# Attention with a cluster mask and an MLP on one Trainium2 core: the value product taken four heads at a time, sums from a pass of ones, and queries in halves

## The chip, the cores and the metric

The kernel runs on one core of one Trainium2 chip. The metric is the device time of one execution in microseconds (us). The core has five engines that run their own instruction lists in order: TensorE (PE; its weight loads are shown as PEld), VectorE (DVE), ScalarE (ACT), GpSimd (POOL) and SyncE (SP), which here only starts transfers. Data is in SBUF and PSUM (128 partitions each; PSUM has eight banks of 512 f32 per partition), and sixteen DMA engines move it.

## The reference

Four batches of eight heads, 768 positions, 64 dimensions, 16 centroids per head. Every query and key is given to the centroid with the largest cosine; a query sees only keys of its own cluster.

```python
q_assign = np.argmax(np.einsum('bhsd,hcd->bhsc', q_n, c_n), axis=-1)
k_assign = np.argmax(np.einsum('bhsd,hcd->bhsc', k_n, c_n), axis=-1)
mask = q_assign[:, :, :, None] == k_assign[:, :, None, :]
scores = scale * np.matmul(q, k.transpose(0, 1, 3, 2))
scores = np.where(mask, scores, -1e9)
attn = np.exp(scores - max); attn = attn / attn.sum(-1)
x = np.matmul(attn, v)                    # to 3072 tokens x 512
h = x @ w_in                              # 512 x 2048
out = (h * sigmoid(h)) @ w_out            # 2048 x 512
```

(The last lines are shortened; all inputs and the output are float32.)

## The kernel before

The order of the work is written out by hand: the tile scheduler is off, and each engine runs what the program emits for it in that order. A head has six key blocks of 128.

**Preparation of a head.** load_qk brings q and k of one head (192 KB each), load_v its v; POOL casts v to f16 into vts (line 83), of which the other 64 columns hold ones. On DVE, hi and lo (lines 91, 97) split q and k, times 128, into a high and a low f16 part; xpose (line 107) transposes both by a DMA into ab, so that a column of ab has the high part in partitions 0 to 63 and the low part in 64 to 127. logits (line 117) multiplies by the centroids: eight matmuls, whose outputs are 32 partitions each, so that q and k in groups of three blocks stand below each other in one PSUM tile. am_t, am_max, am_back (lines 127 to 143) turn it, take the maximum and make a one-hot code, and codes (lines 152, 154) writes the code into partitions 64 to 79 of ab, over the low part: times 16384 for queries, times 16384 minus 16384 for keys. The score matmul over 80 partitions then carries the mask.

**Attention.** A step is one key block j of one head i: qk_mm (lines 163, 164) makes scores for 128 keys and all 768 queries in two matmuls of 512 and 256 columns, exp (line 170) turns them into P on ACT. pv_mm (line 178) multiplies vt (128 columns: 64 of v, 64 of ones) by P, a half of the queries at a time, with six matmuls of 384 columns; half of the output partitions are the value product, the other half the sum of P. evac (line 187) copies it to SBUF on DVE. The sums go through transfers: one row to zt as 128x6, reciprocal there (line 197), out to DRAM (rzd), and back as a broadcast to 64 partitions (rzb, line 206); norm (line 214) on POOL multiplies and writes xt, f16, feature by token, two heads to a tile.

**MLP.** unit_a (line 233) makes 128 of the 2048 hidden features for one half of a batch in four matmuls of 384 columns, with tanh on ACT (line 237) and a product on DVE (line 238), since h sigmoid(h) = h (1 + tanh(h / 2)) / 2; unit_aa (line 252) does the same for both halves at once in the last batch. unit_b (line 272) makes 128 tokens of the output in sixteen matmuls of 512 columns, with a copy on DVE (line 277) and the transfer out.

**Order.** In step j of head i PE gets: the scores of the next step, at j = 3 the logits of head i + 2, a unit A at j = 0, 1, 2, 4, a unit B at j = 5, and three value matmuls of head i - 1 at j = 0, 1, 3, 4. The units of a batch are put in the queue at head 2 of the next batch (so at heads 10, 18, 26). Preparation runs three to six heads ahead. The weights are loaded in eight transfers on POOL's queue (w_load), behind a small copy (pace) that waits for an exp. Fillers (line 296) keep PE running in the first heads. After the last head the rest of the MLP follows.

PSUM: two slots of two banks (st: scores, phs), three of one bank (mm: psL, ph, po), one (pv: pO).

Of the kernel before, what the change touches and what calls it, by code (L numbers as in the profile page):

```python
# [12 lines left out]
ALU = mybir.AluOpType  # L13
AX = mybir.AxisListType


@with_exitstack
def kernel(
# [15 lines left out]
    NT = B * S  # L34
# [3 lines left out]
    NBH = B * H  # L38
    HALF = S // 2
    assert D == 64 and DM == H * D and S == 768 and HC == 16 and H == 8  # L40
# [4 lines left out]
    NV = 8  # L45
# [4 lines left out]
    drpool = ctx.enter_context(tc.tile_pool(name="drpool", bufs=1, space=bass.MemoryType.DRAM))  # L50
# [5 lines left out]
    xts = [const.tile([128, NT], f16, name=f"xt{r}") for r in range(NR)]  # L56
    vts = [const.tile([128, NJ, 128], f16, name=f"vt{n}") for n in range(NV)]
    stk = const.tile([128, H, 32], f16, name="stk")
    ckl = const.tile([128, H, 32], f16, name="ckl")
    ohp = [const.tile([128, 12, 32], f16, name=f"oh{n}") for n in range(2)]  # L60
    pace = const.tile([128, 1], f32, name="pace")
    zz = const.tile([128, 512], f16, name="zz")

    nat, hls, abs_, psLs, LTs, mxs, ohs, Ps, pOs, osbs, zts, rzds, rzbs, pst = ({} for _ in range(14))

    def per_head(f):
        return lambda i, *a: f(i, *a) if 0 <= i < NBH else None

    @per_head
    def load_qk(i):  # L70
        b, h = divmod(i, H)
        qk = mp.tile([128, 2, NJ * D], f32, name="qk", bufs=3)
        nc.sync.dma_start(qk[:, 0, :], q[b, h].rearrange("(p j) d -> p (j d)", j=NJ))
        nc.sync.dma_start(qk[:, 1, :], k[b, h].rearrange("(p j) d -> p (j d)", j=NJ))
        nat[i] = qk

    @per_head
    def load_v(i):
        b, h = divmod(i, H)
        vn = mp.tile([128, NJ, D], f32, name="vn", bufs=3)  # L80
        nc.sync.dma_start(vn, v[b, h].rearrange("(p j) d -> p j d", j=NJ))
        lo = 0 if i % 2 == 0 else 64
        nc.gpsimd.tensor_copy(vts[i % NV][:, :, lo : lo + D], vn)  # L83

    @per_head
    def hi(i, t=slice(0, 2)):
        if i not in hls:
            hls[i] = mp.tile([128, 2 * NJ, 2, D], f16, name="hl", bufs=3)
        hl = hls[i].rearrange("p (t j) c d -> p t j c d", t=2)
        src = nat[i].rearrange("p t (j d) -> p t j d", d=D)  # L90
        nc.vector.tensor_scalar(out=hl[:, t, :, 0, :], in0=src[:, t], scalar1=QS, scalar2=None, op0=ALU.mult)  # L91

    @per_head
    def lo(i, t=slice(0, 2)):
        hl = hls[i].rearrange("p (t j) c d -> p t j c d", t=2)
        src = nat[i].rearrange("p t (j d) -> p t j d", d=D)
        nc.vector.scalar_tensor_tensor(  # L97
            out=hl[:, t, :, 1, :], in0=src[:, t], scalar=QS, in1=hl[:, t, :, 0, :], op0=ALU.mult, op1=ALU.subtract
        )

    @per_head
    def xpose(i, parts=1):
        hl = hls.pop(i)
        ab = mp.tile([128, 2 * NJ, 128], f16, name="ab", bufs=5)
        n = 2 * NJ // parts
        for t in range(parts):
            nc.sync.dma_start_transpose(ab[:, t * n : t * n + n, :], hl[:, t * n : t * n + n].rearrange("p n c d -> p (n c d)"))
        abs_[i] = ab

    @per_head  # L110
    def logits(i):
        h = i % H
        ab = abs_[i]
        psL = ps.tile([128, HALF], f32, name="psL", tag="mm", bufs=3)
        for w, st in ((stk, True), (ckl, False)):
            for g in range(4):
                nc.tensor.matmul(  # L117
                    psL[32 * g : 32 * g + 32, :], w[:, h, :],
                    ab[:, 3 * g : 3 * g + 3, :].rearrange("p n c -> p (n c)"),
                    start=st, stop=not st,  # L120
                )
        psLs[i] = psL

    @per_head
    def am_t(i):
        LT = mp.tile([128, 12, 32], f32, name="LT", bufs=2)
        nc.vector.transpose(LT.rearrange("p n c -> p (n c)"), psLs.pop(i))
        LTs[i] = LT

    @per_head  # L130
    def am_max(i):
        LT = LTs.pop(i)
        mx = mp.tile([128, 12], f32, name="mx", bufs=2)
        nc.vector.tensor_reduce(out=mx, in_=LT[:, :, 0:HC], axis=AX.X, op=ALU.max)
        oh = ohp[i % 2]
        nc.vector.tensor_tensor(
            out=oh[:, :, 0:HC], in0=LT[:, :, 0:HC], in1=mx.unsqueeze(2).to_broadcast([128, 12, HC]), op=ALU.is_ge
        )

    @per_head  # L140
    def am_back(i):
        ohT = mp.tile([128, HALF], f16, name="ohT", bufs=2)
        nc.vector.transpose(ohT, ohp[i % 2].rearrange("p n c -> p (n c)"))
        ohs[i] = ohT

    @per_head
    def codes(i):
        ohT, ab = ohs.pop(i), abs_[i]
        for g in range(4):
            dst = ab[64 : 64 + HC, 3 * g : 3 * g + 3, :].rearrange("p n c -> p (n c)")  # L150
            if g < 2:
                nc.vector.tensor_scalar(out=dst, in0=ohT[32 * g : 32 * g + HC, :], scalar1=OHV, scalar2=None, op0=ALU.mult)
            else:
                nc.vector.tensor_scalar(  # L154
# [364 lines left out]
```

## Time and profile before

| what | us |
|---|---|
| median of three runs | 394.45 |
| the three runs | 393.79, 398.59, 394.45 |
| span of the profiled execution | 393.8 |
| first exp starts | 15.0 |
| first tanh starts | 102.5 |
| last unit B starts its stretch of 96 matmuls | 368.9 |
| DMA queue 1 (loads, transposes, outputs) | 44.29 MB |

The profiled execution took what the fastest of the runs took; its span is that time. The page of the profile gives each engine's busy time, the span in 40 slices (a digit is the busy share in tenths), the chain of work that ended last, and groups of instructions with count, busy time and mean. A matmul's duration has its way through the array in it, so matmuls that follow each other overlap, and their price is read from start to start.

### The profile page before, as it was taken

The page shows a single profiled execution, that of the slowest core. Times are in us where ns is not written, and L with a number is a line of the kernel's source. Part 1 is how long each engine was busy: PE and PEld are TensorE (multiplying, and loading weights), DVE is VectorE, ACT ScalarE, POOL GpSimd, SP SyncE. Part 2 cuts the span into 40 slices and gives each one's busy share as a digit, 9 for nine tenths or more (in the row PEclk, how much of TensorE's full clock was granted, in tenths as well). Part 3 has the DMA queues.
Part 4 walks back from the last instruction along what each step waited for, and adds up shares of the span by engine and source line. Part 5 has one row for each costly group of instructions (what it writes and reads, how often), then busy time and mean ns, then how long its engine had stood idle before and what let it go on. Part 6 is the DMA issues. An engine that isn't in the chain of part 4 may idle for free.

```text
span 393.8 us, 5826 instructions
## 1 busy us (share of the span) xinstructions
PE 344.9 (88%) x2001; PEld 174.6 (44%) x2001; DVE 266.4 (68%) x591; ACT 205.5 (52%) x310; POOL 98.4 (25%) x148
## 2 busy tenths in 40 slices
PE   8759977774687999987999999989999999977995
PEld 3224434432344555543555455445555545443442
DVE  6868877895489987792778877785666345256421
ACT  4337946754477755572666666565557514044300
POOL 3111164365133222222212401250223205000000
PEclk9859989998699999998999999999999999999999
DMA  5796899999868955560555555534310102200022
GB/s 137 189 252 161 198 182 225 195 200 221 144 138 170 227 122 127 130 187 11 147 149 147 123 147 149 145 85 89 87 49 21 49 28 89 80 1 2 1 79 80
DMA packets 82125, 48.84 MB, mean 124 GB/s; under 512 B 62128, under 2 KB 76464, under 8 KB 82096
## 3 DMA queue, kind: packets, MB, share of 16 engines
q1 hardware_dynamic: 79408, 44.29, 46.3%
q0 software_dynamic: 2688, 4.19, 7.0%
q8 instruction: 15, 0.25, 0.3%
q14 instruction: 14, 0.11, 0.1%
HBM read 33.59 MB, written 6.39 MB: 102 GB/s over the span
## 4 chain that ended last, share of the span: by engine, by line
PE 65%; DVE 13%; DMA 12%; ACT 4%; SPq 2%; issue 2%; POOL 1%; DVEq 0%; ACTq 0%; POOLq 0%
PE po L272 21%; PE ph L233 13%; PE pO L178 12%; PE pS L163 8%; DMA qk<-in_k_dram 7%; DMA rzb<-rzd 4%; PE pS L164 3%; PE phs L252 3%; PE junk L296 3%; DVE osb L187 2%; DVE gt L262 2%; DVE gt L238 2%; PE psL L117 2%; DMA rzd<-rz 2%; ACT tn L260 1%
## 5 line engine op out<-in xcount | busy, mean ns | idle before, releaser
L170 ACT ACTIVATE P<-pS 128x768 f16<-128x768 f32 x192 | 149.8, 809 | 34.3 <-PE pS L164 33.8
L237 ACT ACTIVATE tn<-ph 128x384 f32<-128x384 f32 x96 | 47.2, 491 | 102.4 <-PE ph L233 97.3
L178 PE MATMUL pO<-P,vt 128*128 128x384 f16 x384 | 85.7, 334 | 14.9 <-DVE osb L187 14.5
L233 PE MATMUL ph<-xt,win_s 128*128 128x384 f16 x384 | 78.2, 327 | 11.5 <-POOL xt L214 11.5
L272 PE MATMUL po<-wout_s,gt 128*128 128x512 f16 x384 | 87.0, 383 | 0.0
L163 PE MATMUL pS<-ab 80*128 80x512 f16 x192 | 75.9, 396 | 10.0 <-DVE ab L154 5.1
L214 POOL TENSOR_TENSOR xt<-osb,rzb 64x384 f16<-64x384 f32 x64 | 64.3, 1024 | 54.1 <-DMA rzb<-rzd 40.5
L238 DVE SCALAR_TENSOR_TENSOR gt<-tn,ph 128x384 f16<-128x384 f32 x96 | 53.0, 552 | 35.3 <-ACT tn L237 33.4
L178 PEld LDWEIGHTS <-vt 128*128 128x128 f16 x384 | 36.8, 99 | 58.9 <-issue 38.2
L83 POOL CAST vt<-vn 128x384 f16<-128x384 f32 x32 | 18.4, 575 | 174.0 <-DMA vn<-in_v_dram 160.0
L272 PEld LDWEIGHTS <-gt 128*128 128x128 f16 x384 | 38.0, 99 | 44.8 <-issue 2.1
L164 PE MATMUL pS<-ab 80*128 80x256 f16 x192 | 53.6, 279 | 0.0
L277 DVE TENSOR_SCALAR ot<-po 128x512 f32<-128x512 f32 x24 | 16.6, 692 | 53.4 <-PE po L272 53.4
L233 PEld LDWEIGHTS <-win_s 128*128 128x128 f16 x384 | 37.2, 97 | 26.3 <-issue 0.6
L187 DVE COPY osb<-pO 128x384 f32<-128x384 f32 x64 | 35.2, 550 | 2.5 <-PE pO L178 1.9
L97 DVE SCALAR_TENSOR_TENSOR hl<-qk,hl 128x768 f16<-128x768 f32 (+1 forms) x33 | 33.0, 1000 | 0.2
L163 PEld LDWEIGHTS <-ab 80*128 80x128 f16 x192 | 19.0, 99 | 23.0 <-DVE ab L154 6.3
L164 PEld LDWEIGHTS <-ab 80*128 80x128 f16 x192 | 19.4, 101 | 22.1 <-issue 8.3
L91 DVE TENSOR_SCALAR hl<-qk 128x768 f16<-128x768 f32 (+1 forms) x33 | 20.4, 618 | 11.2 <-DMA qk<-in_k_dram 5.8
L252 PE MATMUL phs<-xt,win_s 128*128 128x384 f16 x128 | 22.2, 327 | 5.2 <-DVE gt L262 5.2
L260 ACT ACTIVATE tn<-phs 128x768 f32<-128x768 f32 x16 | 13.0, 811 | 25.0 <-PE phs L252 25.0
L296 PE MATMUL junk<-zz 128*128 128x512 f16 x80 | 24.8, 436 | 1.2 <-DVE zz L312 1.2
(48 smaller groups left out, 199.4 us busy)
## 6 DMA issues: line engine op xcount, KB each, us to landing
qk<-in_q_dram SPq DMA_DIRECT2D x32, 192.0 KB, 3.4
qk<-in_k_dram SPq DMA_DIRECT2D x32, 192.0 KB, 3.2
vn<-in_v_dram SPq DMA_DIRECT2D x32, 192.0 KB, 3.9
rzb<-rzd SPq DMA_DIRECT2D x32, 192.0 KB, 4.0
out_dram<-ot SPq DMA_DIRECT2D x24, 256.0 KB, 2.2
win_s<-in_moe_w_in_dram POOLq DMA_DIRECT2D x4, 512.0 KB, 7.5
wout_s<-in_moe_w_out_dram POOLq DMA_DIRECT2D x4, 512.0 KB, 7.6
ab<-hl SPq DMA_TRANSPOSE x33, 3.8
```

The lines of the kernel that those rows point to most:

```text
L163: nc.tensor.matmul(pS[:, 0:512], lhsT, ab[0:80, 0:4, :].rearrange("p n c -> p (n c)"), start=True, stop=True)
L164: nc.tensor.matmul(pS[:, 512:768], lhsT, ab[0:80, 4:6, :].rearrange("p n c -> p (n c)"), start=True, stop=True)
L170: nc.scalar.activation(out=P, in_=pst.pop((i, j))[:, 0:S], func=AF.Exp, bias=0.0, scale=ESC)
L178: nc.tensor.matmul(pOs[i], vts[i % NV][:, j, :], Ps[i, j][:, c * HALF : c * HALF + HALF], start=(j == 0), stop=(j == NJ - 1))
L187: nc.vector.tensor_copy(osb[:, c * HALF : c * HALF + HALF], pOs.pop(i))
L214: nc.gpsimd.tensor_tensor(out=xts[h // 2][o : o + 64, b * S + c * HALF : b * S + c * HALF + HALF], in0=osbs[i][o : o + 64, cs], in1=rzbs[i ...
L233: nc.tensor.matmul(ph, win_s[:, r, ts(fb, 128)], xts[r][:, T0 : T0 + HALF], start=(r == 0), stop=(r == NR - 1))
L237: nc.scalar.activation(out=tn, in_=ph, func=AF.Tanh, bias=0.0, scale=0.5)
L238: nc.vector.scalar_tensor_tensor(out=gt[:, fb, :], in0=tn, scalar=1.0, in1=ph, op0=ALU.add, op1=ALU.mult)
L252: nc.tensor.matmul(phs[:, 512 * c : 512 * c + HALF], win_s[:, r, ts(fb, 128)], xts[r][:, T0 : T0 + HALF], start=(r == 0), stop=(r == NR - 1),)
L272: nc.tensor.matmul(po, gt[:, fc, ts(t, 128)], wout_s[:, fc, :], start=(fc == 0), stop=(fc == NFB - 1))
L296: nc.tensor.matmul(junk, zz[:, 0:128], zz, start=True, stop=True)
```

## The change

It is a new order of the whole kernel with the same arithmetic for scores and mask.

- **Halves and batches.** A step is now one head, one half c of the queries (384) and two key blocks: two score matmuls of 384 columns, one exp of 768. The order is: batch, half, group of four heads, head, pair of key blocks. So the first half of the queries of all eight heads is done before the second half begins, and k of all eight heads is needed early. There are 192 steps, as before.
- **Value product.** When the twelve steps of a group of four heads and one half are done, pv runs for the group: one pass of 32 value columns, another of the other 32, and one of ones; each pass has six key blocks x four heads = 24 matmuls with a 32-column weight, whose four outputs stand in the four 32-partition groups of one PSUM bank. The pass of ones gives the sums, already repeated over the partitions. rz takes their reciprocal on DVE from PSUM (128x384), and norm multiplies pass and reciprocal on DVE into xt. evac, zt, rzd, rzb and their transfers are gone. In the first two groups the three passes stand in three steps, later in one.
- **MLP rows permuted.** xt's rows are now (head, 32 of its dimensions) per pass, so w_in's rows are loaded in that order (w_load, eight pieces of half the columns, then four of w_out).
- **Jobs.** Preparation is per Job: for batch 0, the first three query blocks and k of a head (nine blocks), and two jobs x with the other query halves of four heads each; later a whole head. raw has 4 buffers, ab 13, P 26, vt 13. The codes run on POOL but for the first job; hi of jobs 1 to 7 runs on ACT.
- **MLP order.** unit_a and quarters of a unit B (part_b, four matmuls) are drawn by a credit: each step may use T = 1.5 us by a table of costs. po has a slot of its own; the slot pv is gone, pO is in mm with psL and ph. The MLP begins at step 27, and the units of a half are put in the queue two steps behind the passes of its second group.

```diff
-                pOs[i], vts[i % NV][:, j, :], Ps[i, j][:, c * HALF : c * HALF + HALF], start=(j == 0), stop=(j == NJ - 1)
+    def pv(b, g, c, what):
+        o = ps.tile([128, 512], f32, name="pO", tag="mm", bufs=3)
+        for j in range(NJ):
+            for h in range(4):
+                i = b * H + 4 * g + h
+                w = ones if what == 2 else vts[i][:, j, EW * what : EW * what + EW]
+                nc.tensor.matmul(
+                    o[32 * h : 32 * h + 32, 0:HALF], w, Ps[i, c, j // 2][:, j % 2, :], start=(j == 0), stop=(j == NJ - 1)
+                )
+    def rz(b, g, c):
+        z = mp.tile([128, HALF], f32, name="rz", bufs=2)
+        nc.vector.reciprocal(z, pvs.pop((b, g, c, 2))[:, 0:HALF])
+    def norm(b, g, c, e):
+        nc.vector.tensor_tensor(
+            out=xts[b, c][:, 2 * g + e, :], in0=pvs.pop((b, g, c, e))[:, 0:HALF], in1=rzs[b, g, c], op=ALU.mult
+        )
...
-        nc.sync.dma_start(rzb[o : o + 64, :], rzds.pop(i).unsqueeze(0).to_broadcast([64, S]))
...
+    units = [
+        (b * H + 4 * g + h, c, m) for b in range(B) for c in range(2) for g in range(2) for h in range(4) for m in range(NM)
+    ]
...
+            src = moe_w_in.rearrange("(g h e d) f -> g e h d f", g=2, h=4, e=2)[g, e][:, :, cs]
+            nc.gpsimd.dma_start(win_s[:, r, cs], src)
...
+    for n, job in enumerate(order):
+        s = 3 * n
+        if n >= 6:
+            put(s - 15, load, job)
+        if n >= 4:
+            put(s - 11, hi, job, "act" if n < 8 else None)
+            put(s - 10, lo, job)
+            put(s - 9, xpose, job)
+        if n >= 2:
+            put(s - 5, logits, job)
+            route(job, s - 5)
...
+    for n in range(12):
+        put(5 + 2 * n if n < 8 else 22 + 3 * (n - 8), w_load, n)
+    for i in range(H, B * H):
+        b, h = divmod(i, H)
+        p = int(24 + 4.5 * h) if b == 1 else 48 * b - 33 + 6 * h
+        put(p - 8, load, job)
+        put(p - 6, load_v, i)
+        put(p - 2, hi, job)
+        put(p - 1, lo, job)
+        put(p, xpose, job)
+        put(p, cast_v, i)
+        put(p + 4, logits, job)
+        route(job, p + 5)
...
+    for s in range(NU + 1):
+        cost = 0.33
+        qk_mm(s + 1)
...
+        for w in blocks:
+            pv(b, g, c, w)
+            cost += 1.0
+            put(s, rz, b, g, c) if w == 2 else put(s, norm, b, g, c, w)
...
+            credit = min(credit + T - cost, 2.0)
+            while credit > 0 or cost < 0.8:
+                got = take(HOLD)
+                if not got:
+                    break
+                credit -= got
+                cost += got
```

In take a unit A counts 0.66 and a quarter of B 0.87; the last four quarters in the queue are held back (HOLD) until more come, and a quarter that ends a tile is followed by at least one step or unit without one. After step 192 the loop over the last half's units (unit_aa, two feature blocks at a time) takes one quarter between each, and the last three tiles follow.

More of the change, by code (lines that the diff above doesn't have):

```diff
@@ L77, in load_v @@
[L77 to L91, printed above, removed]
@@ L110, in logits, with xpose @@
[L110 to L114, printed above, removed]
+    def xpose(job, part=None):
+        s = part or slice(0, job.n)
+        hl = hls[job.name]
+        if job.name not in abs_:
+            abs_[job.name] = mp.tile([128, 12, 128], f16, name="ab", bufs=13)
+        nc.sync.dma_start_transpose(abs_[job.name][:, s, :], hl[:, s].rearrange("p n c d -> p (n c d)"))
+    def logits(job):
+        ab = abs_[job.name]
+        psL = ps.tile([128, 512], f32, name="psL", tag="mm", bufs=3)
@@ new lines, in codes, with load_v, cast_v @@
+    def codes(job, engs=None):
+        for g in range(len(job.groups)):
+            code(job, g, nc.gpsimd if engs is None else engs[g])
+    vts, vns = {}, {}
+    def load_v(i):
+        vn = mp.tile([128, NJ, D], f32, name="vn", bufs=3)
+        nc.sync.dma_start(vn.rearrange("p j d -> p (j d)"), v[i // H, i % H].rearrange("(p j) d -> p (j d)", j=NJ))
+        vns[i] = vn
+    def cast_v(i):
+        vt = mp.tile([128, NJ, D], f16, name="vt", bufs=13)
+        nc.gpsimd.tensor_copy(vt, vns.pop(i))
+        vts[i] = vt
```

593 lines of the change are left out of this document (297 added, 296 removed).

## The prediction

> **What bounds the kernel now.** I read the page's busy times and slices first, then the windows by stage, then the timeline of PE inside a steady stretch, and last the groups for the prices of single instructions.
>
> ```profile
> PE 344.9 (88%) x2001; PEld 174.6 (44%) x2001; DVE 266.4 (68%) x591; ACT 205.5 (52%) x310; POOL 98.4 (25%) x148
> ...
> PE   8759977774687999987999999989999999977995
> ...
> DMA  5796899999868955560555555534310102200022
> ```
>
> The first quarter of the span is another kernel than the rest: PE dips to 4 to 8 tenths and the DMA engines stand at 8 or 9, later PE is at 9 and DMA at 5 or less. The windows put numbers to it (PE, PEld, DVE, ACT and POOL busy, granted clock, DMA share, GB/s):
>
> ```profile
> 0.00:12.00 12.00, 10.81 (x44) 4.24 (x45) 8.22 (x28) 4.40 (x6) 4.68 (x15) 1.00 0.56 150
> 12.00:25.00 13.00, 7.02 (x37) 2.13 (x35) 8.95 (x19) 4.76 (x6) 1.62 (x3) 0.70 0.95 221
> 25.00:50.00 25.00, 22.68 (x136) 11.27 (x137) 21.07 (x52) 18.30 (x23) 3.50 (x6) 0.89 0.91 187
> 50.00:75.00 25.00, 19.79 (x120) 10.15 (x120) 21.02 (x45) 15.29 (x20) 13.99 (x18) 0.93 0.96 196
> 75.00:100.00 25.00, 15.37 (x104) 7.89 (x102) 17.11 (x39) 13.34 (x17) 12.26 (x17) 0.91 1.04 214
> ...
> 200.00:250.00 50.00, 48.55 (x299) 25.31 (x298) 39.10 (x87) 29.96 (x50) 13.15 (x20) 1.00 0.53 135
> ```
>
> From 12 to 100 us the DMA share is 0.91 to 1.04 at about 200 GB/s: the start is bound by transfers. ACT, which does nothing but exp there, is busy 13 to 18 of 25 us. From 200 to 250 us PE is busy 48.55 of 50 us at clock 1.00 and DMA is half idle: PE bounds the rest. Busy time of a pipelined PE says little of a price, so I take prices from start to start in the timeline:
>
> ```profile
> 291.28 0.38 PE L163 MATMUL pS<-ab 80*128 80x512 f16 x1
> 291.50 0.27 PE L164 MATMUL pS<-ab 80*128 80x256 f16 x1
> 291.61 0.81 PE L233 MATMUL ph<-xt,win_s 128*128 128x384 f16 x4
> 292.26 0.65 PE L178 MATMUL pO<-P,vt 128*128 128x384 f16 x3
> 292.75 0.38 PE L163 MATMUL pS<-ab 80*128 80x512 f16 x1
> ...
> 293.95 0.27 PE L164 MATMUL pS<-ab 80*128 80x256 f16 x1
> 294.15 0.35 PE L117 MATMUL psL<-ab,stk 128*32 128x384 f16 x4
> 294.32 0.34 PE L117 MATMUL psL<-ab,ckl 128*32 128x384 f16 x4
> 294.59 0.66 PE L178 MATMUL pO<-P,vt 128*128 128x384 f16 x3
> ...
> 304.73 3.62 PE L272 MATMUL po<-wout_s,gt 128*128 128x512 f16 x16
> 308.18 0.38 PE L163 MATMUL pS<-ab 80*128 80x512 f16 x1
> ```
>
> So the scores of one step (768 columns) take 291.61 - 291.28 = 0.33 us, an MLP unit A (four matmuls) 0.65, a value matmul of 384 columns 0.49 / 3 = 0.163, a whole unit B 3.45 (a quarter of it 0.86). The row that decides the most is that of the logits: four matmuls on 32 columns each start together and the next four start 294.32 - 294.15 = 0.17 us later. Four 32-column matmuls with 384 moving columns cost PE what one full matmul costs. Around them stand 0.09 us before (293.95 + 0.11 to 294.15) and 0.10 behind (294.32 + 0.17 to 294.59): 0.2 per switch to 32 columns and back, and 0.53 for a set of logits.
>
> **PE's work, before and after.** Value product: 384 matmuls x 0.163 = 62.6 us now. After: 16 groups of four heads and one half, three passes each (two of 32 value columns, one of ones), 24 matmuls a pass, four at a time: 6 x 0.163 = 0.98, so 48 x 0.98 = 47, and 20 switches x 0.2 = 4. That saves 11.6. Scores (192 x 0.33), A (128 x 0.65) and B (96 quarters x 0.86) stay, logits go from 32 to 34 sets. The new kernel's PE work is 63 + 51 + 83 + 83 + 18 = 298 us, the old one's some 309. The matmuls alone thus give 11 us; the larger part must come from the 85 us (393.8 - 309) in which PE does nothing useful, and most of that is the start: units A begin at head 10 of 32 now, behind 63 exp steps; after the change, at step 27, since half of the queries of all eight heads is done first.
>
> A page of the Trainium skill speaks against the four at a time. TensorEngine Tiling (Array Packing), Restrictions and Key Properties, says that column tiling disables Fast Weight Load and that a change of mode drains TensorE; TensorE: Matmul & The Clock Gate, Part 3, gives a measured 2.38 times for three column tiles. By that 0.79 a pass would be an estimated 1.23 us, 48 x 0.25 = 12 us more in all; the trace's logits show the full factor and the drain as 0.1 us, and they decide.
>
> **Until step 27.** Prices of the other engines, from the groups:
>
> ```profile
> L214 POOL TENSOR_TENSOR xt<-osb,rzb 64x384 f16<-64x384 f32 x64 | 64.3, 1024 | 54.1 <-DMA rzb<-rzd 40.5 <-DVE gt L238 9.2 <-DVE osb L187 3.7
> L238 DVE SCALAR_TENSOR_TENSOR gt<-tn,ph 128x384 f16<-128x384 f32 x96 | 53.0, 552 | 35.3 <-ACT tn L237 33.4
> L237 ACT ACTIVATE tn<-ph 128x384 f32<-128x384 f32 x96 | 47.2, 491 | 102.4 <-PE ph L233 97.3 <-DVE gt L238 4.0 <-DVE osb L187 1.1
> L187 DVE COPY osb<-pO 128x384 f32<-128x384 f32 x64 | 35.2, 550 | 2.5 <-PE pO L178 1.9
> L97 DVE SCALAR_TENSOR_TENSOR hl<-qk,hl 128x768 f16<-128x768 f32 x31 | 31.9, 1029 | 0.2
> L152 DVE TENSOR_SCALAR ab<-ohT 16x384 f16<-16x384 f16 x64 | 20.8, 325 | 1.5
> L91 DVE TENSOR_SCALAR hl<-qk 128x768 f16<-128x768 f32 x31 | 18.9, 610 | 9.8 <-DMA qk<-in_k_dram 5.8 <-DMA vn<-in_v_dram 3.5
> L83 POOL CAST vt<-vn 128x384 f16<-128x384 f32 x32 | 18.4, 575 | 174.0 <-DMA vn<-in_v_dram 160.0 <-PE pS L164 9.6 <-PE ph L233 4.3
> L143 DVE STREAM_TRANSPOSE ohT<-oh 128x384 f16<-128x384 f16 x32 | 18.4, 575 | 0.7
> L127 DVE STREAM_TRANSPOSE LT<-psL 128x384 f32<-128x384 f32 x32 | 17.5, 546 | 0.0
> L277 DVE TENSOR_SCALAR ot<-po 128x512 f32<-128x512 f32 x24 | 16.6, 692 | 53.4 <-PE po L272 53.4
> L136 DVE TENSOR_TENSOR oh<-LT,mx 128x192 f16<-128x192 f32 x32 | 16.3, 511 | 1.1
> L134 DVE TENSOR_REDUCE mx<-LT 128x12 f32<-128x192 f32 x32 | 10.9, 342 | 0.1
> L197 DVE RECIPROCAL rz<-zt 128x6 f32<-128x6 f32 x32 | 5.9, 184 | 2.8 <-DMA zt<-osb 2.8
> ...
> L338 DVE RECIPROCAL cr<-cy 128x1 f32<-128x1 f32 x2 | 0.3, 163 | 0.0
> ```
> ```profile
> 15.01 0.81 ACT L170 ACTIVATE P<-pS 128x768 f16<-128x768 f32 x1 [7.89 <-PE pS L164]
> ...
> 67.09 4.78 ACT L170 ACTIVATE P<-pS 128x768 f16<-128x768 f32 x6 [2.86 <-PE pS L164]
> ...
> 368.86 20.88 PE L272 MATMUL po<-wout_s,gt 128*128 128x512 f16 x96
> ```
>
> The first exp comes at 15 us and, as the chain ahead of it keeps its links (load, hi and lo, transposes, logits, argmax, codes), I leave it there. Three clocks run then. ACT: 27 steps x 0.80 (six in 4.78) and four casts that it takes over from DVE at some 0.6 (L91): 15 + 24 = 39 us. DVE: for x0, whose codes step 24 needs, the work queued from step 12 is an argmax for k6, k7 and x0 (0.55 + 0.34 + 0.51 + 0.58 = 1.97 each), hi and lo of x0 and x1 (1.64 each), one group's reciprocal and two norms (2.9, below): 12.1 us, where ACT would pass those 12 steps in 9.6: some 3 us late, with POOL's four codes (4 x 0.5 by L83's size) 5 late: 44. DMA: by x0's transpose, eight heads' q half and k (8 x 0.295 MB), their v (8 x 0.197), their transposes (8 x 0.295), x0 and x1 (0.79), x0's transpose (0.39) and six weight pieces (6 x 0.26) have to pass: 9.0 MB. Before moved 12 x 0.150 + 13 x 0.221 = 4.7 MB by 25 us and then 200 GB/s: 25 + 4.3 / 0.2 = 47 us, and logits, argmax and codes behind it (4.5) make 51 for step 24, 54 for step 27. That mix had slow small pieces in it which are gone (sums out, reciprocals out, broadcast in). I take 49, between 44 and 54. w_load is queued on POOL behind codes and casts, so a late head delays weights too; they are needed at 49 only.
>
> **From step 27 to the end PE's program adds up.** Steps 27 to 191 hold 165 scores (165 x 0.33 = 54.5), 13 triples of passes (13 x 3.13 = 40.7), 24 logits (12.7), 112 units A (72.8) and, from the code's credit rule, 74 quarters of B (63.6): 244.3. Behind step 191: the last triple 3.1, a wait of 0.8 for reciprocal and norms, 16 units A 10.4, 22 quarters 18.9: 33.2. From the last matmul to the end before takes 393.8 - (368.86 + 20.88) = 4.1, kept. 49 + 244.3 + 33.2 + 4.1 = 330.6.
>
> Other engines per 12 steps (18 us): ACT 12 x 0.8 + 8 x 0.49 = 13.5. DVE two heads (2 x 3.6), 8 gt 4.4, 1.5 outputs 1.0, two norms 1.1 (by L187, same size from PSUM), one reciprocal: 13.7 + R. POOL loses 64 norms of 1.0 us and gets 126 codes of about 0.5, as much; its casts stay. DVE loses the evacuations (64 x 0.55) and codes (0.3 each). Evacuations, sums, reciprocal writes and broadcasts leave the SP queue.
>
> R, the reciprocal on 128x384 out of PSUM, is in no row. From below it is a plain copy of that size, 0.55; the two reciprocals give (184 - 163) / 5 = 4.2 ns an element, 0.16 + 383 x 0.0042 = 1.77 us, and twice that slope, since six elements are a short run, 3.4. I take 1.77, the slope being measured on the same operation.
>
> Stalls on top: (1) the three PSUM slots mm serve pO, psL and ph. Each triple takes all three, and the next logits or unit A waits for R and a norm; PE runs the other two passes (1.96) and a score meanwhile, so 1.77 is nearly hidden: 13 x 0.3 = 4. Behind that wait the next scores are stuck, and exp with them. (2) po has one slot: 18 times a tile ends in the loop, and the next quarter, 0.66 us on, waits for 0.2 + 0.69 (L277): 18 x 0.3 = 5. (3) Steps 27 to 47 have two A and one piece of a head's preparation each, 1.95 us of DVE against 1.65 of PE, about 12 times: 3. (4) Casts and codes meeting DVE on the way, 3. Together 15 (nothing to 30): **346 us**. The table's runs and the span agree (393.79 and 393.8; the median 394.45), so this needs no shift.
>
> **Rivals.** (a) R is 3.4 us, as an iterative operation might cost. Then every triple holds its slots 1.6 us longer, PE waits about 1.5 in 13 triples and the tail, and DVE is at 17.1 of 18 us with its own lags: 346 + 14 x 1.6 = 368. For it: six elements say little of 384. Against: a slope twice as steep would have made 128x6 take 205 ns, and the row says 184. VectorE: DVE Perf Modes (the Trainium skill, Walkthrough: the 8-slice pipeline) has the reciprocal as a divide with a repeat count of 8; the row lies nearer to half of that, and no run here shows the large size. Chance 0.17.
> (b) The start stays with the DMA queue: all eight heads and the weights by step 27, not six pieces, that is two more pieces (0.52 MB), x1's transpose (0.39) and the loads of two heads of batch 1 (1.18): 2.1 MB or 10.5 us at 200 GB/s. 47 becomes 57.5, step 27 comes at some 61 in place of 49: 358. For it: share 0.95 from 12 us on. Against: nobody needs those by then. Chance 0.15.
> (c) Slower: the four column groups overlap in a short set of eight, but not in 72 pairs of load and matmul in a row, where each load has 0.04 us to hide in. One after another a pass costs 24 x 0.163 = 3.9, and 48 x 2.9 = 140 us come on top: 486. With two at a time it is 48 x 0.98 = 47: 393, a draw, so the rival decides from there. Against it: the second four of the logits, whose weights load while the first run, lose nothing. Chance 0.08, the draw 0.04.
> (d) The earlier start of the MLP brings nothing, since something that I have not seen binds steps 27 to 191, and only the 11 us of matmuls remain: 383. 0.04.
>
> **Numbers.** Forecast 346 with 0.52 (its own range 332 to 360). 330 to 378 also holds (a) and (b), with a little cut off each: about 0.8. A difference under 2%, 7.9 us, can't be told from none; 386.6 is the bound. Faster 0.88 (forecast, a, b, d), same 0.04, slower 0.08.
>
> **What would show it.** Right: four pO matmuls at one start and 0.98 a pass; first tanh near 49 us; PE 9 tenths in every slice from there, with the logits and quarters after a triple under 0.5 us late; DMA share under 0.6 from 100 us. R is read from one row. Wrong: pO fours spread over 0.3 us or more (c); PE waiting on a reciprocal (a); exp waiting on scores held by transfers past 55 us (b). A new wait in the middle, DVE above 90% there, would break the 15 us of stalls.

## The result: 374.2 us, and the profile after

| | before | after |
|---|---|---|
| median of four runs each, us | 394.70 | 374.22 |
| range, us | 393.79 to 398.59 | 373.13 to 381.93 |
| ratio, 95% interval | | 0.944 (0.938 to 0.950) |
| span of the profiled execution, us | 393.8 | 371.4 |

Executions of one kernel fall into a faster and a slower group (after: 373.1 to 374.6 us, and once 381.9); the ratios leave the slower one out, medians and ranges do not, and two profiles below, those of the copy for the reciprocal and of batch 1's preparation later, are of the slower one. The kernel is 22 us faster by the spans, where 48 were forecast. First the page of after: busy times, slices, and the chain of waits that ended last.

```profile
PE 325.2 (88%) x2707; PEld 159.3 (43%) x2707; DVE 246.3 (66%) x409; ACT 208.9 (56%) x325; POOL 138.6 (37%) x180
...
PE   6585536699999999999998999999999999998995
...
PEclk9555565999999999999999999999999999999999
DMA  6989999999763448443736173726350000000012
...
PE po L300 21%; PE ph L266 14%; DMA ab<-hl 11%; PE pS L224 10%; DVE rz L247 7%; PE pO L240 7%; PE psL L113 4%; DVE hl L97 3%; DVE gt L271 3%; PE phs L280 2%; DVE ot L307 2%; DVE LT L123 1%; DVE ohT L146 1%; DVE hl L92 1%; ACT tn L270 1%
```

From slice 9 on (74 us) PE stands at 9 in all but two slices until the last; in before it reached 9 at slice 14, with more dips behind it; DMA is mostly at 4 or less behind 100 us. What did not come is an early start: slices 4 to 8 (28 to 74 us) have PE at 3 to 6 tenths, at half the clock in most, with DMA at 9. The windows cut at the points that the prediction used (columns as before):

```profile
0.00:25.00 25.00, 16.11 (x67) 5.01 (x67) 16.36 (x44) 13.91 (x20) 10.49 (x22) 0.72 0.77 183
25.00:55.70 30.70, 16.16 (x115) 5.17 (x115) 14.80 (x25) 11.06 (x15) 15.64 (x22) 0.56 1.21 153
...
0.00:69.40 69.40, 42.70 (x286) 13.91 (x287) 39.49 (x80) 30.43 (x41) 38.03 (x56) 0.63 1.04 166
...
100.00:325.00 225.00, 215.66 (x1944) 112.14 (x1942) 163.97 (x263) 147.54 (x238) 82.72 (x103) 1.00 0.41 101
```

And the timeline of PE, from the start and from the steady part:

```profile
41.02 0.51 PE L113 MATMUL psL<-ab,stk 128*32 128x384 f16 x3 [7.06 <-DMA ab<-hl]
...
50.51 0.51 PE L113 MATMUL psL<-ab,stk 128*32 128x384 f16 x3 [3.77 <-DMA ab<-hl]
...
55.70 0.51 PE L113 MATMUL psL<-ab,stk 128*32 128x384 f16 x4 [1.92 <-DMA ab<-hl]
...
62.00 0.51 PE L113 MATMUL psL<-ab,stk 128*32 128x384 f16 x4 [3.02 <-DMA ab<-hl]
...
64.15 1.91 PE L240 MATMUL pO<-P,ones 128*32 128x384 f16 x24
...
69.37 0.65 PE L266 MATMUL ph<-xt,win_s 128*128 128x384 f16 x3
...
87.10 1.16 PE L240 MATMUL pO<-P,ones 128*32 128x384 f16 x24
...
183.84 1.16 PE L240 MATMUL pO<-P,ones 128*32 128x384 f16 x24
184.83 2.12 PE L240 MATMUL pO<-P,vt 128*32 128x384 f16 x48
186.88 0.50 PE L224 MATMUL pS<-ab 80*128 80x384 f16 x2
187.66 0.35 PE L113 MATMUL psL<-ab,stk 128*32 128x384 f16 x4 [0.28 <-DVE rz L247]
```

The four logits rows of the start are those of the jobs k6, k7, x0 and x1, and each waits for its transpose (ab from hl). The first unit A is at 69.37 us, forecast 49. In the steady part a pass of 24 matmuls takes 184.83 - 183.84 = 0.99 us, two take 2.05, and the logits behind a triple are 0.28 late.

One mark splits the run: the triple of passes of step 36. It starts at 87.10 us in after. By the prediction's prices (step 27 at 49, then nine steps of 1.65) it should have started at 63.9, with 282.1 us behind it; behind it lie 371.4 - 87.1 = 284.3. **Of the 25 us that the forecast missed, 23 lie ahead of step 36 and 2 behind it.** So the question for the experiments is the start.

### The profile page after: what moved, and what is told of

Read it like the earlier page. It is cut to its first block, busy times and chain, and to the rows that moved or that the text cites. A ratio compares the mean times of both kernels' runs of the same rounds, so it can differ in the third digit from the quotient of the medians.

```text
span 371.4 us, 6949 instructions
## 1 busy us (share of the span) xinstructions
PE 325.2 (88%) x2707; PEld 159.3 (43%) x2707; DVE 246.3 (66%) x409; ACT 208.9 (56%) x325; POOL 138.6 (37%) x180
## 4 chain that ended last, share of the span: by engine, by line
PE 58%; DVE 23%; DMA 13%; issue 2%; ACT 2%; POOL 1%; SPq 1%; DVEq 0%; POOLq 0%; ACTq 0%
PE po L300 21%; PE ph L266 14%; DMA ab<-hl 11%; PE pS L224 10%; DVE rz L247 7%; PE pO L240 7%; PE psL L113 4%; DVE hl L97 3%; DVE gt L271 3%; PE phs L280 2%; DVE ot L307 2%; DVE LT L123 1%; DVE ohT L146 1%; DVE hl L92 1%; ACT tn L270 1%
## 5 line engine op out<-in xcount | busy, mean ns | idle before, releaser
L154 POOL TENSOR_SCALAR ab<-ohT 16x384 f16<-16x384 f16 x63 | 76.8, 1219 | 134.1 <-DVE ohT L146 104.9
L224 PE MATMUL pS<-ab 80*128 80x384 f16 x384 | 99.3, 350 | 5.1 <-POOL ab L156 3.6
L247 DVE RECIPROCAL rz<-pO 128x384 f32<-128x384 f32 x16 | 40.9, 2555 | 16.1 <-PE pO L240 16.1
L156 POOL TENSOR_SCALAR ab<-ohT 16x384 f16<-16x384 f16 x63 | 32.8, 520 | 14.7 <-DVE ohT L146 9.8
L123 DVE STREAM_TRANSPOSE LT<-psL 128x384 f32<-128x384 f32 (+1 forms) x34 | 19.6, 577 | 25.2 <-PE psL L113 25.2
L240 PE MATMUL pO<-P,vt 128*32 128x384 f16 x768 | 36.3, 335 | 0.0
L307 DVE TENSOR_SCALAR ot<-po 128x512 f32<-128x512 f32 x24 | 16.5, 688 | 29.4 <-PE po L300 29.2
L97 DVE SCALAR_TENSOR_TENSOR hl<-raw,hl 128x768 f16<-128x768 f32 (+3 forms) x35 | 31.7, 907 | 0.3
L240 PEld LDWEIGHTS <-vt 128*32 128x32 f16 x768 | 21.0, 99 | 12.2 <-issue 1.8
L146 DVE STREAM_TRANSPOSE ohT<-oh 128x384 f16<-128x384 f16 (+1 forms) x34 | 19.6, 577 | 3.8 <-DVE oh L139 0.5
L240 PE MATMUL pO<-P,ones 128*32 128x384 f16 x384 | 20.3, 350 | 0.0
L92 DVE TENSOR_SCALAR hl<-raw 128x768 f16<-128x768 f32 (+2 forms) x28 | 17.1, 611 | 4.6 <-DMA raw<-in_q_dram 4.5
```

The lines of the kernel that those rows point to most:

```text
L97: nc.vector.scalar_tensor_tensor(out=hl[:, s, 1, :], in0=raws[job.name][:, s, :], scalar=QS, in1=hl[:, s, 0, :], op0=ALU.mult, op1=ALU.sub ...
L154: eng.tensor_scalar(out=dst, in0=src, scalar1=OHV, scalar2=None, op0=ALU.mult)
L156: eng.tensor_scalar(out=dst, in0=src, scalar1=OHV, scalar2=-OHV, op0=ALU.mult, op1=ALU.add)
L224: nc.tensor.matmul(pS[:, e, 0:HALF], abs_[kj.name][0 : 64 + HC, kn, :], rhs, start=True, stop=True)
L240: nc.tensor.matmul(o[32 * h : 32 * h + 32, 0:HALF], w, Ps[i, c, j // 2][:, j % 2, :], start=(j == 0), stop=(j == NJ - 1))
L247: nc.vector.reciprocal(z, pvs.pop((b, g, c, 2))[:, 0:HALF])
```

## The experiments

Two theories of the start. *Weights*: pieces of w_in in flight beside the transposes hold these up, and in-order PE and SP hand the delay on (later put more sharply as *turns*: each packet of a transpose waits behind a packet of the weights). *Volume*: the transfers that the first MLP units need are simply more than the queue moves by then, in whatever order. Beside them stood smaller suspects: GpSimd's codes, the in-order wait for x1, batch 1's early preparation, the reciprocal. Times are medians; after is 374.22. A ratio is against runs of before made beside that kernel (medians of 395.9 to 398.5 us). "Step 36" is the start of its triple in the profiled execution.

**The changed kernel again.** No edit; a measure of the scatter.

> The changed kernel once more, unaltered, as the measure for what runs beside it on this chip: the triple of passes of step 36 at 87 us in the first profile, and 284 us from there to the end. Both theories: the stretch behind step 36 within 2 us of 284; the start may differ from chip to chip, since it is bound by transfers.

Median 377.96 us (373.92 to 381.16), profiled span 373.1, x1's logits at 62.31, step 36 at 88.84, 284.3 us behind it. Here the marks hold to 2 us, but the start can scatter by more: in two runs below whose program is the same up to there, the logits of k7 come at 54.3 us (x1 out of the way) and 55.9 (batch 1 later) for 50.5. So a few us of step 36 in one profile prove nothing alone.

**Weights late.**

```diff
-        put(5 + 2 * n if n < 8 else 22 + 3 * (n - 8), w_load, n)
+        put(19 + n if n < 8 else 28 + 3 * (n - 8), w_load, n)
```

> The eight pieces of w_in are queued at steps 19 to 26 in place of 5 to 19 (w_out at 28 to 37), behind the last transpose of batch 0. Theory A (the late start is the weights' traffic among the transposes of k6, k7, x0 and x1): the logits of x1, at 62.0 us in the changed kernel, come at about 50, since 8 pieces of about 1.6 us DMA time each are out of their way; the first tanh comes at 60 to 64 in place of 71.1, as the units then wait for the weights; time 364 to 368. Theory B (codes on POOL set the pace up to there): x1 stays at 58 to 62 and the time at 371 to 376.

385.04 us, 0.968 (0.962 to 0.974): 11 slower than after, where the theory of the weights had 364 to 368. The timeline of PE:

```profile
47.72 0.51 PE L113 MATMUL psL<-ab,stk 128*32 128x384 f16 x4
...
55.98 0.34 PE L266 MATMUL ph<-xt,win_s 128*128 128x384 f16 x1 [0.93 <-DMA win_s<-in_moe_w_in_dram]
61.01 0.50 PE L266 MATMUL ph<-xt,win_s 128*128 128x384 f16 x1 [4.70 <-DMA win_s<-in_moe_w_in_dram]
68.87 0.50 PE L266 MATMUL ph<-xt,win_s 128*128 128x384 f16 x1 [7.35 <-DMA win_s<-in_moe_w_in_dram]
```

x1's logits come at 47.72 for 62.00 us, with no wait for a transpose: the weights did hold the heads (about 50 was expected). But now they meet the transfers of batch 1, and each matmul of the first unit A waits for a piece of w_in. The delay was moved, not removed.

**Longer rows.** w_in in four pieces of whole rows, 4096 bytes landed a packet for 2048.

```diff
-            nc.gpsimd.dma_start(win_s[:, r, cs], src)
+            nc.gpsimd.dma_start(win_s[:, r, :], src)
```

> w_in in four pieces of whole rows (each a piece of 512 KB at steps 5, 9, 13, 17, rows still permuted) in place of eight half pieces; w_out as it was. If the short rows and their extra 4-byte packets make the traffic slow: DMA moves 180 GB/s or more from 30 to 45 us in place of 124, first tanh before 65, time 366 to 370. If it is only the amount (Theory A): within 1 us of the changed kernel.

390.75 us, 0.983 (0.977 to 0.989), which neither of the two expected: k6's logits wait 13.29 us for 7.06, step 36 is at 105.26. Rows of 2048 bytes are not the trouble; longer ones are worse.

**Codes on GpSimd with two operations.** A surprise of after's groups: the same tile and size costs GpSimd 1219 ns with one operation and 520 with two (L154 is the query's code, L156 the key's); the reciprocal is the third row.

```profile
L154 POOL TENSOR_SCALAR ab<-ohT 16x384 f16<-16x384 f16 x63 | 76.8, 1219 | 134.1 <-DVE ohT L146 104.9
...
L247 DVE RECIPROCAL rz<-pO 128x384 f32<-128x384 f32 x16 | 40.9, 2555 | 16.1 <-PE pO L240 16.1
L156 POOL TENSOR_SCALAR ab<-ohT 16x384 f16<-16x384 f16 x63 | 32.8, 520 | 14.7 <-DVE ohT L146 9.8
```
```diff
-            eng.tensor_scalar(out=dst, in0=src, scalar1=OHV, scalar2=None, op0=ALU.mult)
+            eng.tensor_scalar(out=dst, in0=src, scalar1=OHV, scalar2=0.0, op0=ALU.mult, op1=ALU.add)
```

> The codes of queries on POOL get a second operation (times 16384, plus 0), which changes no value. By the trace the one-operation form takes 1.22 us and the two-operation form 0.52. Theory B: POOL needs 0.7 us less for a head of batch 0 and 1.4 for a later one; the heads from 13 to 31 us pass at 3.2 in place of 3.9 us each, k7's transpose is issued at 32 in place of 35, and the time falls by 3 to 5. Theory A: the gain is given back in the transfers behind, first tanh within 1.5 us of 71, time within 1.5 us of the changed kernel.

378.41 us, 0.953 (0.946 to 0.959), step 36 at 89.61: no gain. The instruction did become cheaper:

```profile
L154 POOL TENSOR_SCALAR ab<-ohT 16x384 f16<-16x384 f16 x63 | 37.5, 595 | 172.9 <-DVE ohT L146 124.0 <-PE pS L224 30.5 <-PE pO L240 9.6
```

**A copy for the reciprocal.** The output is not divided by the sums.

```diff
-        nc.vector.reciprocal(z, pvs.pop((b, g, c, 2))[:, 0:HALF])
+        nc.vector.tensor_copy(z, pvs.pop((b, g, c, 2))[:, 0:HALF])
```

> The reciprocal of the sums is left out: rz copies them (0.55 us by the copy of the kernel before), so that the output is not normalized. The rival of the prediction that makes the reciprocal dear (2.56 us measured, 3.4 there) says 16 to 22 us less. The changed kernel's waits on it sum to 5 us (3.0 logits, 0.9 and 0.9 units), so by the trace 4 to 6 us less: 368 to 370.

369.74 us, 0.928 (0.920 to 0.936), as expected from the trace's waits (368 to 370), and far from the 16 to 22 us of a dear reciprocal. In its profiled execution (376.18 us) step 36 comes only at 99.26, so I compare what lies behind step 36: 374.4 - 99.3 = 275.1 us for 284.3. (A late start does not shorten that stretch: with longer rows step 36 is later still, and 284.2 us lie behind it.) The longest of PE's waits there, first after, then the copy:

```profile
PE ph L266 <- DVE gt L271: 4.1, 8, 0.9
PE psL L113 <- DVE rz L247: 3.0, 9, 0.7
PE psL L113 <- DMA ab<-hl: 1.1, 2, 0.8
```
```profile
PE ph L266 <- DVE gt L271: 2.3, 7, 0.9
PE po L300 <- DVE ot L307: 1.8, 4, 0.7
```

The reciprocal's own waits are 3.0 us; its price behind step 36 is 9.2. All of PE's waits listed there sum to 11.1 us in after and to 4.1 with the copy.

**Half of the weights left out.** The MLP uses the other half twice.

```diff
...
-        put(5 + 2 * n if n < 8 else 22 + 3 * (n - 8), w_load, n)
+        if n in (0, 1, 2, 3, 8, 9):
+            put(5 + 2 * n if n < 8 else 22 + 3 * (n - 8), w_load, n)
```

> Half of the weights are left out (four of eight pieces of w_in, two of four of w_out; the MLP uses the other half twice, so the output is another one). All instructions of PE, ACT and DVE stay. Theory H (the start is bound by the amount that the 16 DMA engines have to move, whatever its order): some 13 us of DMA time are gone by step 36, so its triple comes 9 to 13 us earlier than in the unaltered kernel, and the time falls by as much. Rival (latency of the chain through transposes, POOL's codes and the half clock): under 4 us.

368.22 us, 0.930 (0.924 to 0.937); x1's logits at 56.85, step 36 at 81.44, 5.7 us earlier than in after and 7.4 than in its repeat, between the 9 to 13 and the under 4 expected.

**Batch 1's preparation later.**

```diff
-        p = int(24 + 4.5 * h) if b == 1 else 48 * b - 33 + 6 * h
+        p = int(33 + 3.5 * h) if b == 1 else 48 * b - 33 + 6 * h
```

> The preparation of batch 1 begins nine steps later (int(33 + 3.5 h) in place of int(24 + 4.5 h)), so its loads and transposes are out of the way of batch 0 and the weights; heads are still ready five steps ahead of use. Theory H: three heads' loads (1.9 us each) and two transposes (2.4 each) leave the stretch up to step 36, whose triple comes 6 to 10 us earlier; some of it is lost again in steps 40 to 60 where DVE has a head every 3.5 steps: time 4 to 8 less. Rival: within 2 us.

375.66 us, 0.944 (0.935 to 0.953), step 36 at 88.69: alone it does nothing that shows in the median.

**x1 out of the way.** Its logits and codes at step 29 for 22, since they stand in PE's list ahead of scores that do not need them.

```diff
-            put(s - 5, logits, job)
-            route(job, s - 5)
+            put(s + (2 if n == 9 else -5), logits, job)
+            route(job, s + (2 if n == 9 else -5))
```

> The logits and codes of x1 (the second queries of heads 4 to 7) move from step 22 to step 29; its queries are used from step 36. In the changed kernel PE stands before these logits for 3.0 us with the scores of steps 24 to 35 behind them in the queue. If that wait is what delays the units (a blocked queue), the first unit A comes 4 to 7 us earlier and the time falls by 3 to 6. Theory H: the units start earlier but the weights and the next transposes come no sooner, so step 36 stays within 2 us, and so does the time.

390.35 us, 0.987 (0.979 to 0.994), step 36 at 98.40: neither of the two expected. The first unit A came at 73.6 us, later than in after, since the logits of k7 and x0, which the edit leaves alone, were late themselves (54.3 and 61.6 us for 50.5 and 55.7); at 80 us PE then stood 3.5 us for the transpose of batch 1's first head, whose logits are now ahead of x1's. So the edit did not help, but it does not settle by itself whether the wait for x1 was a mere blockage of the queue.

**Shorter rows.** Each piece takes every other block of 256 columns, so 512 bytes landed a packet for 2048 (a quarter, where the expectation says half); same bytes, same steps.

```diff
-            src = moe_w_in.rearrange("(g h e d) f -> g e h d f", g=2, h=4, e=2)[g, e][:, :, cs]
-            nc.gpsimd.dma_start(win_s[:, r, cs], src)
+            src = moe_w_in.rearrange("(g h e d) (a b c) -> g e b h d a c", g=2, h=4, e=2, b=2, c=256)[g, e, hf]
+            dst = win_s[:, r, :].rearrange("p (a b c) -> b p a c", b=2, c=256)[hf]
+            nc.gpsimd.dma_start(dst, src)
```

> The same pieces of w_in at the same steps, with the same bytes, but each piece takes every other block of 256 columns of its rows, so that its packets are half as long (1 KB read where they were 2 KB). Turns (each 256-byte packet of a transpose waits behind one packet of the weights, so its cost goes with the weights' packet length: 21 ns alone, 75 to 121 ns beside 2 KB, 250 to 355 ns beside 4 KB): the transposes' packets take 45 to 80 ns between 30 and 60 us, the logits of the jobs k6 and k7 wait half as long (about 3.5 and 2 us for 7.06 and 3.77), the triple of step 36 starts 4 to 9 us earlier (78 to 83 for 87.1 us) and the time is 365 to 370. Volume (the bytes and packets of the weights take the transfer engines' time, however they are cut, and short packets move fewer bytes per ns): no earlier, 374 to 382.

382.95 us, 0.963 (0.957 to 0.969), step 36 at 97.05: the time of *turns* missed by 13 us, on the other side. The packets of the trace between 30 and 60 us show what differs (transposes have packets of 256 bytes; time is summed over packets and divided by 16 engines):

```
kernel              transposes: packets, ns each    weights: packets, ns each, us
after                   4209,  63                     726 of 2048 B, 194,  8.8
longer rows             2245, 139                     377 of 4096 B, 341,  8.0
shorter rows            3766,  69                    2476 of  512 B,  79, 12.3 and 5437 of 4 B, 28, 9.4
late two (below)        4259,  24                     606 of 2048 B, 214,  8.1
```

Before the weights come a transpose's packet takes 21 or 22 ns (these four kernels, 5 to 25 us). In the stretch with weights it takes 3 times that on the mean, with long rows 6.6 times; short rows leave it at 69 but keep weights in flight for 21.7 us of engine time in place of some 11 with after's own 4-byte packets. DMA: Bandwidth & Descriptors (the Trainium skill, Queues, rings and completion order) says that each transfer engine takes its queues in turn, a packet at a time. From 2048 to 4096 bytes the rows agree in kind: the transpose's price goes with the length of what is in the other queue. With 512 bytes it did not fall, so length alone does not explain the price, and how the turn is taken the rows do not show.

**Weights late and batch 1 late.** Both edits above together.

> The weights' pieces at steps 19 to 26, behind the transposes of batch 0, and the preparation of batch 1 in slots 33 + 3.5 h for 24 + 4.5 h, so that the two no longer meet; body from step 36 to the end 284 us as in every run so far. Turns: the logits of x1 at 47 to 49 us as with late weights alone, the first unit A at 56 to 60 for 69.4 since the weights have the transfer engines to themselves, step 36 at 72 to 77, the time 358 to 364. Volume: the weights land no sooner than with late weights alone (first unit A 61 us and the units after it held by their pieces), step 36 at 88 to 95, the time 374 to 382.

370.58 us, 0.935 (0.928 to 0.941): x1's logits at 48.05 as *turns* has it, but the first unit A, begun at 57.5, still waits 6.56 us for its weights and step 36 is at 79.65. Each theory has a half.

**Two pieces a step, codes with two operations.** On top of the last kernel.

```diff
...
-        put(19 + n if n < 8 else 28 + 3 * (n - 8), w_load, n)
+        put(19 + n // 2 if n < 8 else 28 + 3 * (n - 8), w_load, n)
```

> As the run with late weights and a late batch 1, but two pieces of the weights a step (steps 19 to 22) and GpSimd's codes in the form with two operations (0.52 us for 1.22). Turns: first unit A at 55 to 59 us, step 36 at 71 to 75, the time 356 to 362: the best of these. Volume: as the run before it within 2 us.

**365.22 us (363.30 to 366.23), 0.919 (0.914 to 0.925): the best of all**, 9 us less than after, if short of the 356 to 362 expected. Two edits at once on the kernel before it: which of them brought the 2.6 us of step 36 isn't told apart. PE's timeline:

```profile
46.41 0.51 PE L113 MATMUL psL<-ab,stk 128*32 128x384 f16 x4 [0.26 <-DMA ab<-hl]
...
48.64 2.11 PE L240 MATMUL pO<-P,ones 128*32 128x384 f16 x24
...
57.16 0.34 PE L266 MATMUL ph<-xt,win_s 128*128 128x384 f16 x1 [2.46 <-DMA win_s<-in_moe_w_in_dram]
61.55 2.64 PE L266 MATMUL ph<-xt,win_s 128*128 128x384 f16 x7 [4.05 <-DMA win_s<-in_moe_w_in_dram]
...
77.03 1.16 PE L240 MATMUL pO<-P,ones 128*32 128x384 f16 x24
```

Freed of the weights, the passes of step 24 begin at 48.64 for 64.15 in after. From the first unit A that runs through, 61.6, to step 36 it is 15.5 us (14.9 in the prediction). Of the 13.1 us by which step 36 still misses its 63.9, waits for w_in are 6.5 (2.46 + 4.05).

**What holds the weights now?** Three edits of the best kernel: batch 1's preparation three slots later still (36 + 3.5 h); that, with four pieces a step from step 18 (18 + n // 4) and w_out from step 32; and the same with half of the weights left out, the MLP using the other half twice.

> The best version so far with nothing altered but batch 1's preparation three steps later (36 + 3.5 h for 33 + 3.5 h): whether batch 1's loads, issued at 44 to 48 us, take the transfer engines from the weights. If they do (2.2 MB ahead of the weights, at 200 GB/s some 5 to 10 us shared): first unit A at 56 to 58 for 61.5 us, the time 358 to 362. If the weights' own packets set it: 61 us, the time 364 to 367.

> The best version so far with its weights a step earlier and four a step (steps 18 and 19, right behind the last transpose of batch 0), batch 1's preparation three steps later (36 + 3.5 h) and w_out from step 32. Overlap (weights beside transposes cost the transposes, weights alone cost only their own transfer): x1's logits at 46 to 49 us as before, the last piece that the first unit A needs lands by 56 for 61.5 us, step 36 at 70 to 74 for 77.0, the time 357 to 362. Volume (the first unit A comes when a fixed number of packets has passed, in whatever order): first unit A not before 60, step 36 at 76 to 80, the time 363 to 368.

> The run before it with half of the weights left out (the MLP uses the other half twice). If the weights' own transfer is what is left of the delay: first unit A within 1 us of the triple's last product (54 to 55 us), step 36 at 66 to 69, the time 351 to 356. If the step order and the half clock of TensorE are: step 36 within 1.5 us of the run before it.

373.16 us, 0.941 (0.936 to 0.947); 372.02, 0.931 (0.921 to 0.940); 370.14, 0.932 (0.927 to 0.937). All are slower than the best, none came to a time that was expected, and step 36 hardly moved: 77.68, 76.95, 75.37 for 77.03. What got worse lies behind it (table). In the second, the four pieces stand on GpSimd ahead of x1's codes, which cost scores 3.5 us. None of the three tested whether batch 1's loads hold the weights: SP, which is not tied to the steps, still issued these loads at 45 to 49 us, beside the weights.

**Loads behind the weights.** So those loads (first three heads of batch 1) went into the weights' own queue, behind w_in, and w_out starts at step 30.

```diff
...
+        q = nc.gpsimd if b == 1 and h < 3 else None
-        put(p - 8, load, job)
-        put(p - 6, load_v, i)
+        put(p - 8, load, job, q)
+        put(p - 6, load_v, i, q)
```

> The best version so far, but the loads of the first three heads of batch 1 (q, k and v, nine transfers, most of them issued at 44 to 49 us and run beside the weights) go into the weights' own queue, behind the eight pieces of w_in, and w_out starts at step 30. If these loads are what holds the weights (they land a median 16.5 us behind their issue): pieces land within 9 to 12 us, the first unit A that is not interrupted starts at 55 to 58 for 61.6 us, step 36 at 70 to 73 for 77.0, the time 358 to 362. If the weights' own packets are: 60 to 62, step 36 at 76 to 78, the time 364 to 368, or more if batch 1 is now late.

370.31 us, 0.936 (0.929 to 0.943). The pieces land in 11.0 us for 16.5, the first unit A runs through from 59.57, step 36 starts at 74.76, between the two expected ranges. So the loads had 2 us of the wait; PE's remaining 4.6 us of waits for w_in come with the weights' own transfers. And batch 1's loads are now late: its first logits wait 5.74 us at 84, and 293.4 us lie behind step 36 for 286.8.

The runs side by side (us):

| kernel | x1's logits | step 36 | behind step 36 | median |
|---|---|---|---|---|
| after | 62.0 | 87.1 | 284.3 | 374.2 |
| after again | 62.3 | 88.8 | 284.3 | 378.0 |
| weights late | 47.7 | 96.5 | 287.8 | 385.0 |
| longer rows | 66.9 | 105.3 | 284.2 | 390.8 |
| codes with two operations | 65.2 | 89.6 | 283.6 | 378.4 |
| copy for the reciprocal | 67.7 | 99.3 | 275.1 | 369.7 |
| batch 1 later | 66.4 | 88.7 | 287.0 | 375.7 |
| x1 out of the way | 82.8 | 98.4 | 289.3 | 390.4 |
| shorter rows | 70.9 | 97.1 | 284.2 | 383.0 |
| half of the weights | 56.9 | 81.4 | 284.2 | 368.2 |
| both late | 48.1 | 79.7 | 287.4 | 370.6 |
| late two (best) | 46.4 | 77.0 | 286.8 | 365.2 |
| batch 1 later still | 47.0 | 77.7 | 293.3 | 373.2 |
| late four | 47.0 | 77.0 | 292.0 | 372.0 |
| late four, half of the weights | 47.2 | 75.4 | 292.7 | 370.1 |
| loads behind | 46.4 | 74.8 | 293.4 | 370.3 |

With the weights late, 2.1 us of what lies behind step 36 are a wait of PE for w_out.

## Why the prediction missed

Faster was right, but the 346 is 28 us off, and 374.2 lies outside the forecast's own 332 to 360; it is inside the 330 to 378 only by the room left there for rivals (a) and (b). By its own steps:

**PE's work: right in sum, in part by luck.** 282.1 us behind step 36 were forecast, 284.3 measured. But the forecast had some 267 of work and 15 of stalls, and of the 284.3 PE's listed waits are 11.1, the rest 273.2: 6 too little and 4 too much nearly cancel. Four groups of columns do run as one: 0.99 us a pass for 0.98. The 1.23 us that stood there as an estimate by the Trainium skill (TensorE: Matmul & The Clock Gate, Part 3) is not seen, nor is rival (c). Rival (d) falls with it; the early MLP brings its gain as soon as it may start.

**R: the size was off, the place was right.** 2.56 us a reciprocal for 1.77 (between the forecast and rival (a)'s 3.4), and its cover holds: logits come 0.3 to 0.7 late after a triple, as the 0.3 of "nearly hidden" had it. But DVE's time lengthens other waits too, so that the copy saves 9.2 us in some 14 triples, 0.66 each, more than the 4 that stall (1) set aside. Rival (a) had put 22 us on top for an R 1.63 longer.

**Until step 27: this failed, in "25 + 4.3 / 0.2 = 47 us".** The volume was nearly right: 183 GB/s by 25 us is 4.6 MB (4.7 in the prediction), and from there to x0's logits at 55.7 us 153 GB/s move 4.7 MB (4.3 in the prediction). The pace was wrong, 153 GB/s for 200: x0 came 8.7 us late. The 200 came from another mix. In before from 25 to 100 us (transfers by queue: packets, MB, share) the weights' queue had a fifth of the engines:

```profile
q1 hardware_dynamic: 24710, 12.33, 75.4%
q0 software_dynamic: 975, 2.50, 20.9%
```

In after it has half in the worst stretch (below). Another 5 us I gave away myself, taking 49 where the clock of the transfers said 54. The remaining 6.7 us passed between x0's logits and the first unit A. PE has x1's logits in its list there, and 3.0 us of it are their wait for one more transpose, which the sum left out. The rest was not told apart; the granted clock is 0.63 there (55.7 to 69.4 us), and scores that were priced at 0.33 us a step take 0.70. 8.7 + 5 + 6.7 = 20.4, which is 69.4 - 49.

**What the pace is made of.** The chain of waits of after, up to 80 us (start, length, link):

```profile
12.41 3.70 DMA ab<-hl
...
35.07 15.39 DMA ab<-hl
...
54.67 7.28 DMA ab<-hl
...
66.33 7.82 DMA ab<-hl
```

A transpose's link takes 3.70 us before the weights come and 15.39 beside them, the rest of the transpose ahead of it in the queue included. And the transfers of after between 30 and 45 us, by queue and by issue (KB, median us to landing):

```profile
q1 hardware_dynamic: 1866, 0.88, 62.4%
q0 software_dynamic: 1542, 0.97, 50.0%
...
win_s<-in_moe_w_in_dram POOLq DMA_DIRECT2D x3, 256.0 KB, 14.5
...
ab<-hl SPq DMA_TRANSPOSE x2, 14.3
```

Shares of 62 and 50% with 1.9 MB in 15 us: the engines are taken, but little moves. That weights beside the transposes are what delays the heads is shown by taking them away: x1's logits at 47.7 for 62.0 us with the weights late (46.4 to 48.1 in all later kernels that have them late), 56.9 with half of them. The prediction looked the wrong way here: "a late head delays weights too; they are needed at 49 only". It is the weights that delay the heads.

**Why the start at 49 was not reached.** Rival (b), "the start stays with the DMA queue", said that heads, weights and two loads of batch 1 (11.1 MB) pass before step 27. By the first unit A 166 GB/s x 69.4 us = 11.5 MB have passed. Its volume was right and its time, 61, too short by the same error of pace. In the best order it does come at 61.6, when 178 GB/s x 61.6 us = 11.0 MB have passed. The orders tried behind that one won at most 2.3 us ahead of step 36 and paid 5 to 7 behind it, where batch 1's preparation came late. So the forecast's step 27 at 49 was out of reach of every order that I ran.

**POOL's codes: mis-sized, free.** 1.22 us for 0.5, but making them 0.6 gained nothing by itself. **"What would show it"** worked: exp and logits held by transfers past 55 us was the sign named for (b), logits behind a triple under 0.5 us late held in part (0.3 to 0.7), and DMA's share behind 100 us is 0.41, below the 0.6 named.

Open: how the transfer engines share out their time between a transpose and weights, and whether an order exists that holds both the weights at 55 us and batch 1's loads in time.

## What to carry to other kernels

A pace read from one mix of transfers does not hold for another: count which queues will be in flight at once, and look up what a transpose or a small packet costs in a stretch where that is so. Loads that are not needed yet are not free when something on the critical chain uses the same engines; put them behind that chain, and look next at what they then delay. Splitting a run at a mark that every variant has (here step 36) shows in one subtraction whether start or body is at fault.

## What the runs showed that I had not expected

- A transpose's 256-byte packet takes 21 ns without weights in flight, 63 on the mean beside 2048-byte packets of weights and 139 beside 4096-byte ones.
- On GpSimd a tensor_scalar of 16x384 f16 takes 1219 ns with one operation, 520 with two and 595 when a second one, adding zero, is put on.
- The reciprocal takes 184 ns for 6 elements a partition and 2555 for 384: (2555 - 184) / 378 = 6.3 ns an element, against 4.2 by the two short rows of before.
